# Retention and a gated FFN: another order for the first loads and the first items

## The chip, the cores and the metric

The kernel runs on one core of a Trainium2 chip. The metric is the device time of one execution in microseconds (us), the median of several runs.

## The reference

Causal retention (attention without softmax, with a decay per head), then two matrix products with `h - tanh(h)` between them:

```python
scores = scale * np.matmul(q, k.transpose(0, 1, 3, 2))        # batch 8, heads 8, seq 576, head_dim 64
Dmat = np.where(rel >= 0, gamma[:, None, None] ** rel[None, :, :], 0.0)   # rel = row - column
attn = np.matmul(scores * Dmat[None], v)
x = attn.transpose(0, 2, 1, 3).reshape(4608, 512)
h = x @ w_in                                                  # 512 x 2048
out = (h - np.tanh(h)) @ w_out                                # 2048 x 512
```

All inputs and outputs are float32.

## The kernel before, in words

The sequence is cut into nine chunks of 64 positions. One batch entry of one chunk is an *item*; eight items (a *chunk*) give a block of 512 tokens for the FFN. The chunks are linked by a state for each batch entry. The FFN works on one block and one tile of 128 hidden units (f, 16 of them) at a time: `mm1` makes a tile h_f by 12 matmuls of 512 columns, `mm2` adds a tile's part to the output.

Every float32 operand of the FFN is split into two words, a high word (`xh`, `gh`) cast on ScalarE and a low word (`xl`, `gl`) that VectorE makes by subtraction; a product is three matmuls. A weight tile is split with more care: it is loaded (`load_w`, 512 KB, tile name rwi), *guarded* (two activations on ScalarE, L106 and L111, into a mask), put together in three VectorE operations (L137, L145, L147; for weight tile 1, in `second`, L124, L126, L127), cast to its high word on ScalarE (L153, L129) and subtracted for the low word (L166). In the text w0, w1, w2 are the weight tiles 0, 1, 2. `unit` is this work for one tile, cut by `yield` into steps that `step()` runs one at a time; `finish` issues the low word that is left over.

The start handles the items of chunk 0 (0 to 7). Each is one load of 384 KB (`load_first`, tile name a). TensorE makes its scores (s_first), VectorE multiplies them by the decay (pm, L308), TensorE makes the output (own_first), ScalarE casts it to xh (L326), VectorE subtracts for xl (L329). Scores of item j+2 are interleaved with the output of item j by `run`. All eight items are needed before h_0, the first FFN tile. Ahead of them TensorE runs *fillers*: matmuls on a zero tile (`busy`, L553).

From chunk 3 on, chunks go in pairs through `stage_a`, which makes an FFN block's products from seven combined weight and input variants (`product`), for pairs j of hidden tiles. Its sums go through `u2` and `u4` on VectorE to c22, c12 and c21, with one piece of the first pair (`rest`) left for the second pair in a list, `pending`.

The order is written by hand: `in_order` ties each engine's instructions to the order in which the code issues them. All loads but two go out on SP's queue, strictly in order, over eight completion semaphores (DMAHW0 to 7). Some loads are *paced*: `paced` notes the instruction issued last, and `behind` makes a load wait until that instruction is done.

Of the kernel before, what the change touches and what calls it, by code (L numbers as in the profile page):

```python
# [13 lines left out]
AF = mybir.ActivationFunctionType  # L14
ALU = mybir.AluOpType
PSUM = bass.MemoryType.PSUM

B, H, S, D = 8, 8, 576, 64
# [11 lines left out]


STEP = float(np.arctanh(0.5) / (1.06 * 2.0**-15))
WARM = 24

NI = NC * B
NV = 7
# [38 lines left out]
def retention_ffn(ctx: ExitStack, tc: tile.TileContext, ins, out, spill, wvar):  # L75
# [36 lines left out]

    halves = (slice(0, DM // 2), slice(DM // 2, DM))

    def second(low):

        t, f = stream[1]
        hw, lw, z = wraw[t, f][:, :, 1], wraw[t, f][:, :, 0], masks.pop((t, f))
        del wraw[t, f]

        w = const.tile([P, 2, 2, DM // 2], F32R, tag="wi14", name="wi1")
        win[f] = w
        upto("guard", 3)
        nc.vector.scalar_tensor_tensor(z, hw, 3, z, op0=ALU.logical_shift_left, op1=ALU.bitwise_and)  # L124
        low()
        nc.vector.scalar_tensor_tensor(z, lw, 29, z, op0=ALU.logical_shift_right, op1=ALU.bitwise_or)  # L126
        nc.vector.scalar_tensor_tensor(z, hw, -0x40000000, z, op0=ALU.bitwise_and, op1=ALU.bitwise_or)  # L127
        for n, at in enumerate(halves):
            nc.scalar.copy(w[:, n, 0], z[:, at].bitcast(F32))  # L129
        last.append(("i", w, z))  # L130
# [32 lines left out]
    def finish():  # L163
        while last:
            hi, lo, full = words_of(*last.pop())
            nc.vector.tensor_tensor(lo, full, hi.bitcast(F32), op=ALU.subtract)  # L166
# [7 lines left out]
    def upto(what, n):  # L174
        while at_[what] < min(n, 2 * NF):
            {"load": load_w, "guard": guard}[what](*stream[at_[what]])
            at_[what] += 1
# [106 lines left out]
    def m_out(j, o, state_last=False):  # L284
        c0, b = divmod(j, B)
        a, pm = loaded[j], scored[j]
        ms = []
        for i in range(4):
            two = [[(o[half(1 - c), i], a[half(c), 2, i, :], pm[half(c), i, :]) for c in range(2)]]
            if c0 > 0:  # L290
                two.insert(state_last, [(o[half(1 - c), i], state[half(c), b, i, :], a[half(c), 0, i, :]) for c in range(2)])
            ms += [(*m, k == 0, k == len(two) - 1) for k, terms in enumerate(two) for m in terms]
        return ms

    def run(same, other):

        while same or other:
            for ms in (same, other):
                for out_, w, x, start, stop in ms[:2]:
                    nc.tensor.matmul(out_, w, x, start=start, stop=stop)  # L300
                del ms[:2]

    def after_score(j, sc, n):

        if j < B:

            pm = pool.tile([P, 2, 4, C], F32, tag="gh", name=f"pm{j}")
            nc.vector.tensor_tensor(pm[:, 0], sc[:, 0], decay, op=ALU.mult)  # L308
        else:

            pm = parts[j, 0][:, :, 1]
            nc.vector.tensor_tensor(
                pm, sc, mask.unsqueeze(1).unsqueeze(1).broadcast_to([P, n, 4, C]), op=ALU.mult,
            )
        for u in range(n):
            scored[j + u] = pm[:, u]
# [234 lines left out]
    def busy(n, cols):  # L551
        for _ in range(n):
            nc.tensor.matmul(wps[:, :cols], warm[:, :P], warm[:, :cols], start=True, stop=True)  # L553

    busy(WARM, 140)
    busy(8, BLK // 2)
    decay = const.tile([P, 4, C], F32, tag="wo7", name="decay")
    krows = [const.tile([P, 4, 4, D], F32, tag=f"wo{4 + t}", name=f"krows{t}") for t in range(2)]

    def load_first(j, queue=nc.sync):  # L560
        loaded[j] = const.tile([P, 3, 4, C], F32, tag=f"wo{NF - 1 - j}", name=f"a{j}")
        queue.dma_start(loaded[j], first_d[j])

    load_first(0)
    nc.scalar.dma_start(decay, decay_d)
    load_first(1, nc.scalar)
    load_first(2)
    upto("load", 1)
    load_first(3)
    load_first(4)  # L570
    load_first(5)
    nc.scalar.activation(warm[:, :1], warm[:, :1], AF.Tanh)

    firsts, lows = {}, []

    def score_first(j):
        firsts[j] = psp.tile([P, 8, C], F32, tag=("o0", "o1", "h")[j % 3], bufs=(1, 1, 2)[j % 3], name=f"s_first{j}")
        firsts[j] = firsts[j][:, :4]  # L580
        return m_score(j, firsts[j])

    def paced(load):

        pace.append(tc.nc.cur_bb.bb.instructions[-1].name)
        load()

    def load_paced(j):
        load_first(j)
        behind(tc, pace[-1])  # L590

    run(score_first(0), [])
    after_score(0, firsts[0].unsqueeze(1), 1)
    run(score_first(1), [])
    after_score(1, firsts[1].unsqueeze(1), 1)
    for j in range(B):
        o = psp.tile([P, 8, C], F32, tag=("o2", "o3", "own")[j % 3], bufs=1, name=f"own_first{j}")[:, :4]
        run(score_first(j + 2) if j < B - 2 else [], m_out(j, o))
        if j == 0:
            paced(lambda: load_paced(6))  # L600
        if j == 1:
            paced(lambda: load_paced(7))
        if j < B - 2:
            after_score(j + 2, firsts[j + 2].unsqueeze(1), 1)
            if 0 < j < 5:
                paced(lambda: upto("load", j + 1))
        if j == 4:
            nc.sync.dma_start(vtab, vtab_d)
            nc.sync.dma_start(krows[0], krows_d[0])
            load_pair(B)  # L610
            nc.sync.dma_start(mask, mask_d)
            upto("load", 7)
            load_pair(B + 2)
        if j == 3:
            busy(6, BLK)
        if 0 < j < 4:
            step()
        low = after_out(j, o.unsqueeze(1), 1, False)
        if j == 0:
            upto("guard", 1)  # L620
        if j == 3:
            step()
        if j == 5:
            finish()
            guard(*stream[1], both=False)
        if j < 7:
            low()
        else:
            guard_end(masks[stream[1]])
            at_["guard"] = 2  # L630
    units(1)
    second(low)
    at_["convert"] = 2

    def scale_k(t):
# [319 lines left out]
    def stage_a(na):  # L955

        nb, pending = na + 1, []
        u2, u4 = work[:, 0], work[:, 1]
        for j in range(NPAIR):
            x, y = [psp.tile([P, BLK], F32, tag=t, bufs=1, name=f"p{t}{na}_{j}") for t in ("new" if j else "o0", "own")]  # L960
            z, v = [psp.tile([P, BLK], F32, tag="h", bufs=2, name=f"p{t}{na}_{j}") for t in "zv"]
            f1, f2 = 2 * j, 2 * j + 1
            c22, c12, c21 = [pool.tile([P, BLK], F32, tag="g", bufs=3, name=f"c{t}_{na}_{j}") for t in (22, 12, 21)]

            def tanh(c):
                th = pool.tile([P, BLK], F32, tag="cv", bufs=4, name=f"th{na}_{j}")
                nc.scalar.activation(th, c, AF.Tanh)  # L967
                return th

            def away(c, f):  # L970
                nc.gpsimd.tensor_tensor(c, c, tanh(c), op=ALU.subtract)  # L971
                nc.sync.dma_start(spill[nb, f], c)

            product(0, x)
            product(1, y)
            nc.scalar.copy(u2, x)
            nc.vector.tensor_tensor(u2, y, u2, op=ALU.add)  # L977
            product(2, z)
            nc.vector.tensor_tensor(u4, z, u2, op=ALU.add)
            while pending:  # L980
                pending.pop()()
            product(3, v)
            nc.vector.tensor_tensor(c22, v, u4, op=ALU.add)  # L983
            y = psp.tile([P, BLK], F32, tag="own", bufs=1, name=f"py{na}_{j}")
            product(4, y)
            away(c22, f2)
            nc.vector.tensor_tensor(c12, y, u4, op=ALU.add)
            product(5, x, False)
            away(c12, f1)
            g11 = tanh(x)  # L990
            nc.vector.tensor_tensor(g11, x, g11, op=ALU.subtract)
            product(6, v, False)
            split(na, f1, g11, False)
            nc.vector.tensor_tensor(c21, v, u2, op=ALU.add)

            def rest(f=f2, c=c21, tanh=tanh):
                nc.vector.tensor_tensor(c, c, tanh(c), op=ALU.subtract)
                split(na, f, c, True)

            if j == 0:  # L1000
                pending.append(rest)
            else:
                mm2_pair(na, j - 1)
                rest()
        for f in range(3):
            fetch(nb, f)
        mm2_pair(na, NPAIR - 1)
        for f in range(2):
            split(nb, f, fetched.pop((nb, f)), False)
# [123 lines left out]
```

## Time and profile before

| | us |
|---|---|
| median of 3 runs (lowest to highest) | 854.9 (854.4 to 855.17) |
| profiled execution | 856.53 |
| its span, first to last instruction | 854.8 |
| TensorE busy in the span | 843.2 |
| VectorE busy | 484.6 |
| ScalarE busy | 364.4 |

In the profile's rows PE is TensorE's matmuls, PEld its weight loads, DVE VectorE, ACT ScalarE, SPq the queue that issues loads. A row of the timeline has the start, the time taken, the engine, the line, the operation with output and inputs, and in brackets how long the engine stood idle before it and what ended that. A row of a group has its count and the mean time of one. A row of DMA issues has the size and the time from issue to landing. Line numbers are those of the kernel before; in the changed kernel they lie up to ten lower.

### The profile page before, as it was taken

How to read it: one execution, taken by the hardware profiler on the slowest of the kernel's cores; microseconds unless marked ns; L12 is line 12 of the kernel's file. 1: busy time of each engine (PE TensorE's matmuls, PEld its weight loads, DVE VectorE, ACT ScalarE, POOL GpSimd, SP SyncE). 2: the span in 40 equal slices, each digit the busy share in tenths (PEclk: the TensorE clock that was granted, in tenths of full speed). 3: DMA queues.
4: the chain of work that ended last, by engine and by line, in shares of the span. 5: the costliest groups of instructions: out<-in, count | busy, mean ns of one | idle time of the engine just before them, and what ended most of it. 6: DMA issues, size and time to landing. Idle time of an engine off the chain costs nothing.

```text
span 854.8 us, 18569 instructions
## 1 busy us (share of the span) xinstructions
PE 843.2 (99%) x7701; PEld 695.2 (81%) x7702; DVE 484.6 (57%) x817; ACT 364.4 (43%) x723; POOL 74.3 (9%) x63
## 2 busy tenths in 40 slices
PE   7999999999999999999999999999999999999998
PEld 6888888887888787888888788888888888888886
DVE  5989877868567665434346754434456554343321
ACT  4887774444234553323244443322345433232321
POOL 0001001110000001212110002211100012121100
PEclk9999999999999999999999999999999999999999
DMA  9976968776777579435376665534666255352432
GB/s 340 364 244 205 365 222 277 239 235 202 234 259 289 188 252 326 163 130 190 123 235 213 205 184 199 182 132 173 208 207 215 90 184 185 128 192 74 138 109 74
DMA packets 62404, 174.67 MB, mean 204 GB/s; under 512 B 7536, under 2 KB 8944, under 8 KB 57072
## 3 DMA queue, kind: packets, MB, share of 16 engines
q1 hardware_dynamic: 61792, 172.57, 59.5%
q8 instruction: 60, 0.98, 0.5%
q10 hardware_dynamic: 528, 0.92, 0.3%
q14 instruction: 24, 0.20, 0.1%
HBM read 124.70 MB, written 48.76 MB: 203 GB/s over the span
## 4 chain that ended last, share of the span: by engine, by line
PE 87%; issue 4%; DMA 4%; DVE 2%; ACT 1%; SPq 0%; POOL 0%; DVEq 0%; POOLq 0%; ACTq 0%
PE o L503 25%; PE o L948 15%; PE h L447 15%; PE pv L917 7%; PE pnew L917 6%; PE py L917 4%; PE pz L917 4%; PE pown L917 4%; PE s L300 3%; DMA s<-spill_dram 2%; PE new L300 2%; PE own L300 2%; DMA a<-in_first_dram 1%; PE po L917 1%; DMA rwi<-in_w_in_dram 1%
## 5 line engine op out<-in xcount | busy, mean ns | idle before, releaser
L503 PE MATMUL o<-wo,gh 128*128 128x512 f32 x608 | 156.8, 395 | 0.3 <-ACT gh L484 0.3
L503 PEld LDWEIGHTS o<-wo,gh 128*128 128x128 f32 x608 | 111.8, 188 | 26.8 <-ACT gh L484 2.2
L971 POOL TENSOR_TENSOR c<-c,th 128x512 f32<-128x512 f32 x48 | 62.0, 1297 | 516.6 <-ACT th L967 515.5
L967 ACT ACTIVATE th<-c 128x512 f32<-128x512 f32 x72 | 45.5, 632 | 140.9 <-DVE c L983 89.7
L447 PE MATMUL h<-xh,wi 128*128 128x512 f32 x384 | 97.7, 392 | 0.8 <-ACT xh L326 0.5
L447 PEld LDWEIGHTS h<-xh,wi 128*128 128x128 f32 x384 | 71.3, 188 | 16.9 <-ACT wi L129 0.8
L503 PE MATMUL o<-wo,gl 128*128 128x512 f32 x304 | 84.2, 389 | 0.0
L948 PE MATMUL o<-wo,gs 128*128 128x512 f32 x288 | 70.7, 389 | 0.0
L503 PEld LDWEIGHTS o<-wo,gl 128*128 128x128 f32 x304 | 57.1, 188 | 11.9
L948 PEld LDWEIGHTS o<-wo,gs 128*128 128x128 f32 x288 | 54.1, 188 | 11.2
L917 PE MATMUL pv<-xhv,ws 128*128 128x512 f32 x192 | 59.2, 390 | 0.6 <-DVE c L983 0.6
L503 PE MATMUL o<-wo,gs 128*128 128x512 f32 x240 | 59.2, 394 | 0.0
L300 PE MATMUL own<-qk,state 64*64 64x64 f32 x928 | 57.1, 221 | 0.0
L300 PE MATMUL own<-qk,vr 64*64 64x64 f32 x928 | 56.1, 218 | 0.7 <-issue 0.7
L977 DVE TENSOR_TENSOR work<-pown,work 128x512 f32<-128x512 f32 x24 | 16.6, 692 | 67.8 <-PE pown L917 67.1
L503 PEld LDWEIGHTS o<-wo,gs 128*128 128x128 f32 x240 | 44.4, 188 | 9.5
L917 PE MATMUL pnew<-xhv,ws 128*128 128x512 f32 x168 | 51.7, 389 | 0.0
L447 PE MATMUL h<-xl,wi 128*128 128x512 f32 x192 | 51.6, 389 | 0.0
L948 PE MATMUL o<-wo,gh 128*128 128x512 f32 x192 | 48.9, 389 | 0.0
L300 PEld LDWEIGHTS own<-qk,vr 64*64 64x64 f32 x928 | 46.6, 135 | 0.1
L300 PEld LDWEIGHTS own<-qk,state 64*64 64x64 f32 x928 | 46.2, 134 | 0.4 <-issue 0.4
L933 DVE TENSOR_TENSOR gl<-s,gh 128x512 fp32r<-128x512 f32 x44 | 30.0, 688 | 23.9 <-ACT gh L932 12.1
(152 smaller groups left out, 1516.4 us busy)
## 6 DMA issues: line engine op xcount, KB each, us to landing
ws<-wvar_dram SPq DMA_DIRECT2D x41, 1024.0 KB, 4.7
s<-spill_dram SPq DMA_DIRECT2D x94, 256.0 KB, 3.8
qk<-in_qkv_dram SPq DMA_DIRECT2D x29, 512.0 KB, 4.2
vr<-in_qkv_dram SPq DMA_DIRECT2D x29, 512.0 KB, 3.9
spill_dram<-c SPq DMA_DIRECT2D x48, 256.0 KB, 2.3
spill_dram<-g SPq DMA_DIRECT2D x36, 256.0 KB, 3.5
rwi<-in_w_in_dram SPq DMA_DIRECT2D x16, 512.0 KB, 5.6
rwo<-in_w_out_dram SPq DMA_DIRECT2D x16, 512.0 KB, 5.5
```

The source lines that it names most:

```text
L300: nc.tensor.matmul(out_, w, x, start=start, stop=stop)
L447: nc.tensor.matmul(hp, win[f][:, cc // 2, a, cc % 2 * P : (cc % 2 + 1) * P], x[:, cc, :], start=(k == 0), stop=(k == 3 * NCC - 1))
L503: nc.tensor.matmul(ops[n][t], g[:, t * P : (t + 1) * P], wout[f_][:, a, :], start=(f_ == first and k == 0), stop=(f_ == final and k == 2),)
L917: nc.tensor.matmul(into, w[:, a, k], x[:, k], start=start and i == 0, stop=i == len(terms) - 1, skip_group_check=not start,)
L933: nc.vector.tensor_tensor(gl, g, gh.bitcast(F32), op=ALU.subtract)
L948: nc.tensor.matmul(ops[n][t], g[:, t * P : (t + 1) * P], wout[f][:, a, :], start=(j == 0 and f == fs[0] and k == 0), stop=last_,)
L967: nc.scalar.activation(th, c, AF.Tanh)
L971: nc.gpsimd.tensor_tensor(c, c, tanh(c), op=ALU.subtract)
L977: nc.vector.tensor_tensor(u2, y, u2, op=ALU.add)
```

## The change

Six edits. At the start, weight tile 0 is loaded first of all on SP and items 0 to 5 behind it, all on SP's queue (item 1 was on ScalarE's); the order was item 0, item 2, weight tile 0, items 3 to 5. The fillers ahead of the items become 11 of 512 columns instead of 24 of 140 and 8 of 256, and the 6 fillers after item 3's output go. Weight tile 0's guard and conversion steps move ahead of and between items 0 to 2. Item 7's scores are issued whole, ahead of item 5's output, instead of interleaved with it. The pacing marks move: they are taken before `after_score` instead of behind it. A tanh on one column that loaded ScalarE's table early goes, and the low word of each item is issued at once. In `stage_a`, c22 is computed ahead of what is pending, and `u2` alternates between two places.

```diff
-WARM = 24
+WARM = 11
...
-    busy(WARM, 140)
-    busy(8, BLK // 2)
+    busy(WARM, BLK)
...
-    load_first(0)
+    upto("load", 1)
     nc.scalar.dma_start(decay, decay_d)
-    load_first(1, nc.scalar)
-    load_first(2)
-    upto("load", 1)
-    load_first(3)
-    load_first(4)
-    load_first(5)
-    nc.scalar.activation(warm[:, :1], warm[:, :1], AF.Tanh)
...
+    for j in range(6):
+        load_first(j)
+    upto("guard", 1)
...
     run(score_first(0), [])
+    step()
     after_score(0, firsts[0].unsqueeze(1), 1)
     run(score_first(1), [])
+    step()
     after_score(1, firsts[1].unsqueeze(1), 1)
     for j in range(B):
         o = psp.tile([P, 8, C], F32, tag=("o2", "o3", "own")[j % 3], bufs=1, name=f"own_first{j}")[:, :4]
-        run(score_first(j + 2) if j < B - 2 else [], m_out(j, o))
-        if j == 0:
-            paced(lambda: load_paced(6))
-        if j == 1:
-            paced(lambda: load_paced(7))
-        if j < B - 2:
-            after_score(j + 2, firsts[j + 2].unsqueeze(1), 1)
-            if 0 < j < 5:
-                paced(lambda: upto("load", j + 1))
+        if j == 5:
+            run(score_first(7), [])
+            run([], m_out(j, o))
+        else:
+            run(score_first(j + 2) if j < B - 2 else [], m_out(j, o))
+        if j < 2:
+            paced(lambda: load_paced(6 + j))
+        if 0 < j < 5:
+            paced(lambda: upto("load", j + 1))
...
-        if j == 3:
-            busy(6, BLK)
-        if 0 < j < 4:
+        if j == 0:
             step()
-        low = after_out(j, o.unsqueeze(1), 1, False)
+        if j < B - 2:
+            after_score(j + 2, firsts[j + 2].unsqueeze(1), 1)
+        after_out(j, o.unsqueeze(1), 1)
         if j == 0:
-            upto("guard", 1)
-        if j == 3:
             step()
+        if j == 1:
+            finish()
...
-        u2, u4 = work[:, 0], work[:, 1]
+        u4 = work[:, 1]
         for j in range(NPAIR):
+            u2 = work[:, 3 * (j % 2)]
...
+            product(3, v)
+            nc.vector.tensor_tensor(c22, v, u4, op=ALU.add)
             while pending:
                 pending.pop()()
-            product(3, v)
-            nc.vector.tensor_tensor(c22, v, u4, op=ALU.add)
```

Three places in the engines' order. First SP's queue, which issues the loads, from item 6 on, before (a_161 and a_190 are items 6 and 7, rwi_194 to rwi_244 the weight tiles 1 to 3; what a load waits for stands in brackets):

```order
L562 DMA a_161<-in_first_dram 128x768 [waits DMAHW0_49,PE_49]
L562 DMA a_190<-in_first_dram 128x768 [waits DMAHW1_49,PE_49]
L96 DMA rwi_194<-in_w_in_dram 128x1024 [waits DMAHW2_49,DVE_49]
L96 DMA rwi_219<-in_w_in_dram 128x1024 [waits DMAHW3_49,DVE_49]
L96 DMA rwi_244<-in_w_in_dram 128x1024 [waits DMAHW4_49,DVE_49]
```

The same place of the change (a_144 and a_173 are items 6 and 7, rwi_175 to rwi_224 the weight tiles 1 to 3):

```order
L560 DMA a_144<-in_first_dram 128x768 [waits DMAHW0_49,PE_49]
L560 DMA a_173<-in_first_dram 128x768 [waits DMAHW1_49,PE_49]
L96 DMA rwi_175<-in_w_in_dram 128x1024 [waits DMAHW2_49,DMAHW1_49]
L96 DMA rwi_200<-in_w_in_dram 128x1024 [waits DMAHW3_49,PE_49]
L96 DMA rwi_224<-in_w_in_dram 128x1024 [waits DMAHW4_49,PE_49]
```

The loads stand in the same order; weight tile 1 waited for a VectorE instruction and now waits for DMAHW1, on which the load of item 7 reports (weight tile 0's was the one before it there), and tiles 2 and 3 wait for TensorE instead of VectorE.

Second, ScalarE behind item 5's output, before (xh_165 is the block's high word, mi_320 the mask of weight tile 1) and then of the change (xh_149, mi_293):

```order
L326 CAST xh_165<-own_first_298 128x4x64 [waits PE_49]
L106 ACTIVATE mi_320<-rwi_194 128x512 [waits DMAHW2_49]
L326 CAST xh_165<-own_first_323 128x4x64 [waits PE_49]
L326 CAST xh_165<-own_first_334 128x4x64 [waits PE_49]
L111 ACTIVATE mi_320<-mi_320 128x512 [waits Activation_49]
```

```order
L325 CAST xh_149<-own_first_271 128x4x64 [waits PE_49]
L106 ACTIVATE mi_293<-rwi_175 128x512 [waits DMAHW2_49]
L325 CAST xh_149<-own_first_295 128x4x64 [waits PE_49]
L325 CAST xh_149<-own_first_306 128x4x64 [waits PE_49]
L111 ACTIVATE mi_293<-mi_293 128x512 [waits Activation_49]
```

Nothing moved here: in both, the guard of weight tile 1 stands ahead of the casts of items 6 and 7.

Third, VectorE in the second pair (1) of the first `stage_a`, before and of the change (c_3_0_4089 and c_3_0_4061 are the first pair's c21, c_3_1_4160 and c_3_1_4132 the second pair's c22):

```order
L977 TENSOR_TENSOR work<-pown_1_4157,work 128x512 [waits PE_49,Activation_49]
L979 TENSOR_TENSOR work<-pz_1_4158,work 128x512 [waits DVE_49,PE_49]
L997 TENSOR_TENSOR c_3_0_4089<-c_3_0_4089,th_1_4186 128x512 [waits Activation_49]
L933 TENSOR_TENSOR gs<-c_3_0_4089,gs 128x512 [waits Activation_49]
L983 TENSOR_TENSOR c_3_1_4160<-pv_1_4159,work 128x512 [waits DVE_49,PE_49]
```

```order
L968 TENSOR_TENSOR work<-pown_1_4129,work 128x512 [waits PE_49,Activation_49]
L970 TENSOR_TENSOR work<-pz_1_4130,work 128x512 [waits DVE_49,PE_49]
L972 TENSOR_TENSOR c_3_1_4132<-pv_1_4131,work 128x512 [waits DVE_49,DMAHW5_49,PE_49,Pool_49]
L988 TENSOR_TENSOR c_3_0_4061<-c_3_0_4061,th_1_4165 128x512 [waits Activation_49]
L923 TENSOR_TENSOR gs<-c_3_0_4061,gs 128x512 [waits Activation_49]
```

c22 moved ahead of the two pending instructions, and now also waits for the store of the first pair's c22 out of its buffer.

More of the change, by code (lines that the diff above doesn't have):

```diff
@@ L113, in retention_ffn, with second @@
     halves = (slice(0, DM // 2), slice(DM // 2, DM))
-    def second(low):
+    def second():
         t, f = stream[1]
@@ L124, in second @@
         nc.vector.scalar_tensor_tensor(z, hw, 3, z, op0=ALU.logical_shift_left, op1=ALU.bitwise_and)
-        low()
         nc.vector.scalar_tensor_tensor(z, lw, 29, z, op0=ALU.logical_shift_right, op1=ALU.bitwise_or)
@@ L562, in load_first @@
         queue.dma_start(loaded[j], first_d[j])
-    load_first(0)
+    upto("load", 1)
     nc.scalar.dma_start(decay, decay_d)
-    load_first(1, nc.scalar)
-    load_first(2)
-    upto("load", 1)
-    load_first(3)
-    load_first(4)
-    load_first(5)
-    nc.scalar.activation(warm[:, :1], warm[:, :1], AF.Tanh)
-    firsts, lows = {}, []
+    for j in range(6):
+        load_first(j)
+    upto("guard", 1)
+    firsts = {}
     def score_first(j):
@@ L613, in retention_ffn @@
             load_pair(B + 2)
-        if j == 3:
-            busy(6, BLK)
-        if 0 < j < 4:
+        if j == 0:
             step()
-        low = after_out(j, o.unsqueeze(1), 1, False)
+        if j < B - 2:
+            after_score(j + 2, firsts[j + 2].unsqueeze(1), 1)
+        after_out(j, o.unsqueeze(1), 1)
         if j == 0:
-            upto("guard", 1)
-        if j == 3:
             step()
+        if j == 1:
+            finish()
         if j == 5:
-            finish()
             guard(*stream[1], both=False)
[L626 to L632, printed above, removed]
+    guard_end(masks[stream[1]])
+    at_["guard"] = 2
+    assert not going and not last
+    second()
     at_["convert"] = 2
```

## The prediction

> **What bounds the kernel now.** I read the page first, then who TensorE waits for, then the chain of waits through the start, then single stretches of the engines.
>
> ```profile
> PE 843.2 (99%) x7701; PEld 695.2 (81%) x7702; DVE 484.6 (57%) x817; ACT 364.4 (43%) x723; POOL 74.3 (9%) x63
> q8 instruction: 60, 0.98, 0.5%
> qk<-in_qkv_dram SPq DMA_DIRECT2D x29, 512.0 KB, 4.2
> spill_dram<-c SPq DMA_DIRECT2D x48, 256.0 KB, 2.3
> ```
>
> TensorE is busy for 99% of the span, so an edit pays only where TensorE stands still. The waits of TensorE over the whole span (us in total, times, longest) say where that is:
>
> ```profile
> PE s_first L300 <- DMA a<-in_first_dram: 2.9, 5, 1.3
> ...
> PE pv L917 <- DVE c L983: 0.6, 1, 0.6
> PE h L447 <- ACT xh L326: 0.5, 1, 0.5
> PE h L447 <- ACT wi L129: 0.3, 1, 0.3
> ```
>
> All but one lie in the first 20 us; the other, for c22, is the one that the last hunk of the diff touches. What sets the end of the start? The chain of waits (start, us, what):
>
> ```profile
> 2.13 6.55 DMA a<-in_first_dram
> ...
> 9.59 0.44 DVE pm L308
> 10.04 5.13 DMA rwi<-in_w_in_dram
> 15.20 0.68 ACT mi L106
> 15.88 0.54 ACT xh L326 x2
> 16.41 0.54 ACT mi L111
> 16.98 0.69 DVE mi L124
> 17.67 0.33 DVE xl L329
> 18.00 0.61 DVE mi L126
> 18.64 0.70 DVE mi L127
> 19.36 0.41 ACT wi L129
> 19.82 3.01 PE h L447 x12
> 22.84 5.79 PE h L447 x24
> ```
>
> This is not the chain of weight tile 0. It is that of weight tile 1 (w1): loaded from 10.04, landed at 15.17, guarded on ScalarE, put together by three operations of VectorE, cast, and used by h_1 at 19.82. From there TensorE runs on without a gap, so the start of h_1 is what has to come earlier. TensorE's own timeline before it:
>
> ```profile
> 14.05 0.27 PE L300 MATMUL s_first<-a 64*64 64x64 f32 x2 [0.41 <-DMA a<-in_first_dram]
> ...
> 14.52 1.44 PE L300 MATMUL own_first<-pm,a 64*64 64x64 f32 x34
> 16.47 2.11 PE L447 MATMUL h<-xh,wi 128*128 128x512 f32 x8 [0.51 <-ACT xh L326]
> 18.42 1.07 PE L447 MATMUL h<-xl,wi 128*128 128x512 f32 x4
> ```
>
> h_0 starts at 16.47, 1.30 after w1 landed, and that is no accident: on ScalarE the first guard of w1 (15.20) stands ahead of the casts xh of items 6 and 7, so h_0 cannot start before w1 has landed either.
>
> **The change part by part.** *Tile 0 first, items behind it.* Only the order of the first 3.8 MB changes. Ahead of item 3 there were decay, items 0 to 2 and w0, and there still are, so item 3 lands at 8.68 as in the chain's first row. Item 0 lands later by w0's 512 KB, and w0 earlier; its guard and its three VectorE operations move into the waits for items 0 to 2, where VectorE has room. What w0 was late for was nothing: h_0 waited for xh. Worth 0, and hidden by the loads of the items.
>
> *The load of w1.* Here is the price. Before, its issue waited for VectorE's third pm (9.59 plus 0.44, hence 10.04). Now the pacing mark is taken right behind the load of item 7, so the mark is that load, and w1 may not be issued before item 7 has landed. The loads of w2, w3, w4 and all that SP issues later are queued behind it on SP, ScalarE's casts of items 6 and 7 behind w1's guard, and h_0 and h_1 behind those. When does item 7 land, and how long does w1 then take? SP's issues of items 6 and 7, the landing time of item 6, and all transfers up to 12.0 us:
>
> ```profile
> 8.16 0.33 SPq L562 DMA_DIRECT2D a<-in_first_dram  x1
> ...
> 9.58 0.33 SPq L562 DMA_DIRECT2D a<-in_first_dram  x1
> ...
> a<-in_first_dram SPq DMA_DIRECT2D x1, 384.0 KB, 3.5
> ...
> DMA packets 1431, 3.82 MB, mean 318 GB/s; under 512 B 153, under 2 KB 281, under 8 KB 1430
> q8 instruction: 1, 0.02, 0.6%
> ```
>
> Item 7 is issued when item 1's output is computed, behind item 3's landing: 9.6 in both. Late bound of its landing: 14.05, where TensorE got it before. Early bound: by 12.0 us 3.82 MB had moved, and decay, w0 and eight items are 3.80 MB, so its bytes were nearly all across; item 6 landed at 8.16 + 3.5 = 11.66, and 384 KB at 318 GB/s take 1.2, which gives 12.9. That it took 1.1 longer I put down to the one instruction packet in the window: the page has 60 of them, 0.98 MB, for 15,403 instructions of TensorE, so 16 KB, some 257 instructions, and a packet occupies one of 16 engines. It comes by count. Now 54 TensorE instructions fewer stand ahead (21 fillers of two fewer at the start, 6 in the middle), which puts it into item 4's run, behind most of item 7's bytes. So I take 13.1, nearer the early bound.
>
> w1 then meets an idle queue. The nearest rows are the loads of 512 KB later in the program, median 4.2 for qk on the page, and for vr:
>
> ```profile
> DMA to landing us min/median/max: 3.3/3.9/8.1
> ```
>
> Bounds 3.3 and 4.2; I take 3.6, since nothing else is in flight. w1 lands at 13.1 + 3.6 = 16.7 (early 12.9 + 3.3 = 16.2, late 14.05 + 4.2 = 18.25), against 15.17.
>
> The Trainium skill, "DMA: Bandwidth & Descriptors", section "Anatomy of one DMA", gives a fixed 2.0 us plus the bytes over 436 GB/s, of which most is the receipt after the last byte. By it w1 would take an estimated 3.2, and the sum below would come out 0.4 lower; the shortest row here, 3.3, agrees with it nearly.
>
> From w1's landing to h_1 it was 19.82 - 15.17 = 4.65. The xl at 17.67 now stands ahead of the chain; two spacings of 0.70 (18.64 to 19.34) take the place of 1.02 and 0.64 behind L124, so about 0.2 goes: 4.45. h_1 starts at 16.7 + 4.45 = 21.15, later by **1.3** (early 20.65, +0.8; late 22.7, +2.9). h_0 starts at 16.7 + 1.3 = 18.0 and ends 2.85 later, just ahead of h_1, so it is not the bound. Since TensorE has no gap behind h_1 that could take this in, it stays to the end. w2 to w4 now go out in a row behind w1, and VectorE needs four operations of 0.69 for a tile against TensorE's 5.79 for two, so the tiles stay ahead.
>
> *Item 7's scores ahead of item 5's output, six fillers gone.* TensorE waits for w1 in both; scores earlier make pm 7 earlier, 0 on the path. The same for the warm-up: 24 of 140 and 8 of 256 columns are 5,408, 11 of 512 are 5,632, and item 0 now lands after the fillers' end.
>
> *c22 sooner.* The second pair of the first variant stage, VectorE and then TensorE:
>
> ```profile
> 337.78 0.68 DVE L997 TENSOR_TENSOR c<-c,th 128x512 f32<-128x512 f32 x1
> 339.15 0.69 DVE L933 TENSOR_TENSOR gs<-c,gs 128x512 fp32r<-128x512 f32 x1 [0.69 <-ACT gs L932]
> 339.95 0.69 DVE L983 TENSOR_TENSOR c<-pv,work 128x512 f32<-128x512 f32 x1
> ...
> 339.08 0.62 PE L917 MATMUL pnew<-xlv,ws 128*128 128x512 f32 x2
> 339.53 0.61 PE L917 MATMUL pnew<-xhv,ws 128*128 128x512 f32 x2
> 340.69 0.73 PE L917 MATMUL pv<-xhv,ws 128*128 128x512 f32 x2 [0.55 <-DVE c L983]
> 341.26 0.63 PE L917 MATMUL pv<-xlv,ws 128*128 128x512 f32 x2
> ```
>
> Pairs of matmuls follow each other by 0.45 (339.08, 339.53); the pair at 341.26 was due at 340.44, so the wait costs 0.8. With c22 first it takes L997's place at 337.8 and is done at 338.5, 1.5 us before it is needed. It now also waits for the first pair's c22 to leave its buffer: that was made seven products of 1.36 earlier, and the store takes 2.3 (the page), which leaves 7 us for the tanh and the subtraction between: 0. The gs behind it moves to about 340.4, and mm2 needs it at 342.2 less 0.7: covered by 1.1. The second home for u2 takes a wait of ScalarE's copy away that TensorE does not see: 0. **-0.8**, in this stage alone; the waits list has no second one.
>
> **Sum.** +1.3 - 0.8 = +0.5. The profiled execution took 856.53 us, 854.8 of it the span; its time becomes 857.0. It lies 1.6 above the median of the three runs, 854.9, so the median becomes **855.4**.
>
> **The rivals.** *TensorE goes cold before h_0 (slower).* The place is the wait between item 7's output and h_0. Item 7's scores to the last output took 14.05 to 15.96, so the new idle time reaches from about 15.0 to 18.0, 3 us, with no filler left in it; before it was 0.5. What a slow clock costs is in the fillers:
>
> ```profile
> 1.19 3.86 PE L553 MATMUL wps<-warm 128*128 128x140 bf16 x32 [1.19 <-DVE warm L547]
> ...
> 11.53 1.24 PE L553 MATMUL wps<-warm 128*128 128x512 bf16 x5 [0.16 <-issue]
> ```
>
> The later ones stream 2,560 columns in 1.24, 2.1 per ns; the first 5,408 took 3.86, 1.4 per ns, which half speed for some 2.8 us and full speed for the rest would make (an estimate). For h_0's matmuls of 0.23 half speed adds 0.2 each, over 2.8 us up to all 12: 1.3 to 2.4, less the 0.3 by which h_0 ends ahead of h_1. With 1.5 the sum is +2.0: 856.9. It decides once an idle time is long enough for the drop; the longest here, 1.3 us in the waits for items, did no harm, and no row shows a longer one: chance 0.12. The Trainium skill, "TensorE: Matmul & The Clock Gate", section "Part 1: The HAM clock gate", speaks against the change here: a free-running window of about 3.4 us that is idle halves the clock. By it 3 us would still pass, narrowly, and 855.4 would stand.
>
> *Item 7 lands as late as before, and w1 takes the median (slower).* The instruction packet hits the same transfer: +2.9 - 0.8 = +2.1, 857.0. For it: 14.05 is the only landing that was seen. Chance 0.10.
>
> *All is early (same).* +0.8 - 0.8 = 0.0: 854.9, and 854.5 with the spread of the runs. Part of the forecast's side, 0.2.
>
> *c22 sooner does nothing*, since something else than the order on VectorE held it: +1.3, 856.2. The spacing of VectorE's rows speaks against it: 0.06.
>
> *Faster.* 1.7 us would need w1 in place before 14.5, which the wait for item 7 excludes, or a gain in a stage where TensorE does not wait. I see none: 0.08.
>
> **How the numbers follow.** Forecast 0.44, with all-early and c22-without-effect 0.70; these lie within 0.2% (1.7 us), about what a measurement can tell. Slower by more: 0.12 + 0.10 = 0.22. Faster: 0.08. The range goes from 854.0, below the early case by the runs' spread, to 857.6, which takes in the late case and most of the cold one.
>
> **What would show it.** Right: w1's issue directly behind item 7's landing, near 13; DMA engines idle between 13 and 14; h_0 at about 18 and h_1 at about 21; the wait for c22 gone. Wrong: w1's issue near 10, or h_1 before 20.5; a lower spacing than 0.23 in h_0 would be no cold clock, 0.43 would be one; a wait of pv in the second pair that is still there.

## The result and the profile after

The changed kernel takes 859.3 us (median of six runs, 858.3 to 863.6), the kernel before 854.4 us on the same chip (854.0 to 855.2). The ratio is 1.0056, with a 95% interval of 1.0038 to 1.0074: **slower by about half a percent**. The prediction, 855.4 with a range of 854.0 to 857.6, was wrong. The profiled execution of the change took 858.73 us, 856.9 of it the span, against 856.53 and 854.8 before.

TensorE's row on the first part of the page of the change shows that no work was added; the waits of TensorE (us in total, times, longest) show what was:

```profile
PE 842.8 (98%) x7675; PEld 695.2 (81%) x7675; DVE 484.4 (57%) x817; ACT 365.6 (43%) x722; POOL 75.4 (9%) x63
```

```profile
PE s_first L299 <- DMA a<-in_first_dram: 3.4, 7, 1.5
PE h L446 <- ACT xh L325: 2.6, 1, 2.6
PE new_first L299 <- issue: 1.5, 1, 1.5
...
PE new L299 <- issue: 0.9, 2, 0.6
```

Two rows stand out. The wait of h for the cast xh was 0.5 and is 2.6. The wait at new_first, 1.5 us with no releaser that the profile shows ("issue"), did not exist. The row of pv behind c22 (0.6 before) is gone. The waits for items grew from 2.9 to 3.4.

The chain of waits through the start of the change (start, us, what):

```profile
9.95 4.27 DMA a<-in_first_dram
...
14.24 3.61 DMA rwi<-in_w_in_dram
...
17.87 0.66 ACT mi L106
18.53 0.54 ACT xh L325 x2
19.07 0.04 issue
19.11 12.80 PE h L446 x48
```

Item 7 lands at 14.22, and w1 is issued in the same moment, at 14.24; before it was issued at 10.04. Its load takes 3.61 and lands at 17.85. Then comes the guard, the casts, and h_0 at 19.11. But the chain does not go on as before. There it went through the VectorE work on w1 to h_1. Here it enters TensorE at h_0 and stays: 12.80 us for 48 matmuls, so TensorE itself is late. The one-microsecond windows say why (core; from:to; busy time and instructions of PE, PEld, DVE, ACT, POOL; then granted clock, DMA share, GB/s):

```profile
13.00:14.00 1.00, 0.00 (x0) 0.00 (x0) 0.76 (x2) 0.30 (x1) 0.00 (x0) 1.00 0.06 22
14.00:15.00 1.00, 0.64 (x28) 0.67 (x29) 0.00 (x0) 0.00 (x0) 0.00 (x0) 1.00 0.00 0
...
17.00:18.00 1.00, 0.00 (x0) 0.00 (x0) 0.00 (x0) 0.13 (x1) 0.00 (x0) 1.00 0.98 393
...
19.00:20.00 1.00, 0.89 (x3) 0.76 (x4) 0.95 (x3) 0.59 (x2) 0.00 (x0) 0.81 1.03 410
20.00:21.00 1.00, 1.00 (x3) 0.72 (x3) 0.97 (x2) 0.75 (x2) 0.00 (x0) 0.50 0.98 393
...
22.00:23.00 1.00, 1.00 (x4) 0.81 (x3) 0.82 (x2) 1.00 (x3) 0.00 (x0) 0.50 1.03 394
23.00:24.00 1.00, 1.00 (x5) 0.80 (x5) 0.96 (x3) 0.97 (x3) 0.00 (x0) 0.98 1.02 397
```

Three things stand in these rows. From 13 to 15 the DMA engines do nearly nothing, which is the hole ahead of w1. In the 17:18 window TensorE does nothing. And half a microsecond after h_0 begins, at 19.63, the granted clock falls to 0.50 and stays there until 23.04. TensorE's timeline shows what that does to h_0, and when h_1 begins (at 23.57):

```profile
19.11 3.37 PE L446 MATMUL h<-xh,wi 128*128 128x512 f32 x8 [2.57 <-ACT xh L325]
22.28 1.44 PE L446 MATMUL h<-xl,wi 128*128 128x512 f32 x4
23.57 0.62 PE L446 MATMUL h<-xh,wi 128*128 128x512 f32 x2
```

Eight matmuls take 3.37 where they took 2.11. From the start of h_0 to that of h_1 it is 4.46, against 3.35 before.

Following the same matmul through both traces, the change is later by 2.65 us at h_0, by 3.75 at h_1, by about 5 behind the stall at new_first, by 2.65 at 339 us, since pauses of 0.2 to 0.7 at other places fall differently in the two executions, by 1.78 behind c22, and by 2.2 at the end of the span. The medians lie 4.9 apart. The profiled execution of before was itself 2.1 slower than the median of the six runs, and that of the change 0.6 faster than its own, so the two traces show less than half of the loss.

### The profile page after: what moved, and what is told of

Same layout as the page of the kernel before. It is cut to its first block, busy times and chain, and to the rows that moved or that the text cites. A ratio compares the mean times of both kernels' runs of the same rounds, so it can differ in the third digit from the quotient of the medians.

```text
span 856.9 us, 18511 instructions
## 1 busy us (share of the span) xinstructions
PE 842.8 (98%) x7675; PEld 695.2 (81%) x7675; DVE 484.4 (57%) x817; ACT 365.6 (43%) x722; POOL 75.4 (9%) x63
## 4 chain that ended last, share of the span: by engine, by line
PE 97%; DMA 2%; issue 0%; ACT 0%; SPq 0%
PE o L502 31%; PE h L446 16%; PE o L938 15%; PE pv L907 8%; PE pnew L907 7%; PE py L907 4%; PE pz L907 4%; PE pown L907 4%; PE s L299 3%; PE new L299 2%; PE own L299 2%; DMA a<-in_first_dram 1%; PE po L907 1%; PE new_first L299 0%; DMA rwi<-in_w_in_dram 0%
```

## The experiments

The two theories were these. **A**: the time went where the prediction put it, into the load of w1 that now waits for item 7, only more of it. **B**: the clock fell, because TensorE had too little to do before h_0, through that wait or through the six fillers that are gone. A third cause joined them after the first profiles: **C**, the new stall at new_first, from instructions that arrive late. All ratios are against the kernel before on the same chip, with 95% intervals. Each run lists the mean granted clock of every execution, and that counts the drops roughly: 3.4 us at half speed take 0.002 off it, and a drop in the last 2 us of the kernel up to 0.001 more. The profiles with one stretch at half speed ahead of that have 0.997 or 0.998, those with two 0.996, those with three 0.994 or 0.993.

### e1_mark: the change, with w1 issued as early as before

```diff
-        if 0 < j < 5:
+        if j == 1:
+            upto("load", 2)
+        if 1 < j < 5:
             paced(lambda: upto("load", j + 1))
```

> The change, but the load of weight tile 1 (w1) is marked by item 1's output on TensorE, not by item 7's load. Theory A (w1's wait for item 7's landing is the cause, the cold clock follows from it): w1 issued near 10.4, landed near 15.4, h_0 at 16.7, h_1 at 19.9, clock 1.00 throughout, and with c22 sooner 0.9 below before: 853.5 us, ratio 0.999. Theory B (the fillers that were taken out let the clock drop, whatever w1 does): the granted clock still drops to 0.5 around h_0, some 856 to 858 us, ratio 1.002 to 1.004.

Measured: 1.0045 (1.0029 to 1.0061), no better than the change. The edit did what it says: w1 was issued at 10.52. But item 7 now landed at 15.66, and w1 at 16.92. The waits of TensorE and two-microsecond windows of e1_mark:

```profile
PE s_first L299 <- DMA a<-in_first_dram: 5.8, 8, 2.8
...
PE new_first L299 <- issue: 1.9, 1, 1.9
```

```profile
12.00:14.00 2.00, 0.69 (x32) 0.59 (x32) 1.73 (x5) 0.73 (x2) 0.00 (x0) 1.00 0.87 237
14.00:16.00 2.00, 0.21 (x4) 0.24 (x6) 0.00 (x0) 0.00 (x0) 0.00 (x0) 0.56 0.85 284
16.00:18.00 2.00, 2.00 (x48) 2.00 (x48) 0.55 (x2) 0.55 (x2) 0.00 (x0) 0.50 0.95 371
...
20.00:22.00 2.00, 2.00 (x8) 1.53 (x8) 1.84 (x3) 1.26 (x3) 0.00 (x0) 0.73 1.06 396
```

TensorE waits up to 2.8 for an item, has 0.69 and 0.21 us of work in four, and the clock falls ahead of item 7's scores. It stays low from 14.25 to 21.07. Behind the stall at new_first it fell a second time, from 55.21 to 58.62. So A alone is not it: with w1 out of its wait the loss is the same, and the profile has the clock and the stall in its place. Every one of its ten executions had a mean clock of 0.998 or less, and here the times go with it: the five at 0.997 or 0.998 took 857.0 to 859.9, the five at 0.996 or less 859.9 to 862.6. In e9_late and e10_change, below, no such order shows.

### e2_fill: the change, with twelve fillers ahead of h_0

```diff
     second()
+    busy(12, BLK)
```

> The change, with 12 fillers of 512 columns (2.6 us) between item 7's output and h_0; w1 still waits for item 7's landing. Theory A: h_0 stays at 19.1, warm; h_1 goes from 23.6 to 22.3 (w1's landing 17.9 plus 4.45); 2.5 late less 0.9: some 856.0, ratio 1.002. Theory B: the whole loss goes, 853.5 to 854.4, ratio 0.999 to 1.000.

Measured: 1.0048 (1.0032 to 1.0064). h_0 ran warm here (its eight matmuls took 2.19), yet nothing was won, and the trace says why: the clock had already fallen at 15.24, in the wait for item 7, where no filler stood; item 7's outputs ran at half speed, and the twelve fillers behind them ended at 20.5 us, where w1's landing at 18.30 plus the 1.26 that h_0 takes from it in the change would have made 19.56. The fillers held h_0 back themselves by a microsecond. Two of the four executions had a mean clock of 0.999 and 1.000, and they took 860.4 and 859.5, no less than the others. The run does not tell A from B; its twelve fillers are used again in e8_warm, where the clock is held from the beginning.

### e3_wait: the kernel before, with w1 behind item 7

```diff
             paced(lambda: load_paced(7))
+            paced(lambda: upto("load", 2))
...
-            if 0 < j < 5:
+            if 1 < j < 5:
                 paced(lambda: upto("load", j + 1))
```

> The kernel before with one edit: w1's load waits for item 7's landing. All fillers stay, the six after item 3 too. Theory A: w1 lands near 17.8, the idle time before h_0 is some 2 to 3 us and the clock drops in part of the runs: h_1 at 22.3 to 23.6, 856.9 to 858.2, ratio 1.003 to 1.0045. Theory B: the six fillers hold the clock, and what is left is the late tile alone: at most 856.9, no row of the clock below 1.00.

Measured: 1.0053 (1.0033 to 1.0074), the whole loss of the change from this one edit, in four executions. All fillers of before are there. The waits of TensorE in e3_wait:

```profile
PE h L447 <- ACT xh L326: 4.6, 1, 4.6
```

w1 was issued at 14.90 and landed at 20.22, h_0 began at 21.49 after 4.6 us without work, the clock was 0.5 from 18.77 to 25.60, and h_1 began at 26.25.

### e4_c22: the kernel before, with the second pair's c22 sooner

```diff
-        u2, u4 = work[:, 0], work[:, 1]
+        u4 = work[:, 1]
...
+            u2 = work[:, 3 * (j % 2)]
...
+            product(3, v)
+            nc.vector.tensor_tensor(c22, v, u4, op=ALU.add)
             while pending:
                 pending.pop()()
-            product(3, v)
-            nc.vector.tensor_tensor(c22, v, u4, op=ALU.add)
```

> The kernel before with the last hunk alone (c22 ahead of what is pending, u2 in two places). If the order on VectorE held c22: the wait of pv for c22 in the second pair is gone, 0.8 to 0.9 less: 853.5, ratio 0.999. If something else held it: the wait stays, ratio 1.000.

Measured: 1.0002 (0.9992 to 1.0013). The wait of pv for c22 is gone from its list, and the same matmul's distance from the kernel before shrinks by 0.86 us at 339 us. In the change it shrinks by 0.87; VectorE's row there, and TensorE's (start, length):

```profile
340.19 0.69 DVE L972 TENSOR_TENSOR c<-pv,work 128x512 f32<-128x512 f32 x1 [0.74 <-PE pv L907]
```

```profile
342.18 0.61 PE L907 MATMUL pnew<-xhv,ws 128*128 128x512 f32 x2
342.63 0.62 PE L907 MATMUL pv<-xhv,ws 128*128 128x512 f32 x2
```

c22 is done at 340.88, and the pairs of matmuls follow each other by 0.45 without a hole. 0.86 us is 0.1%, and the interval is as wide as that, so the time can't show it. The gain is not always there to be had, either: in e3_wait, where c22 stands in its old place, the wait is not in the list at all, since TensorE came to that place later against VectorE. VectorE's row of e3_wait, and TensorE's:

```profile
343.63 0.69 DVE L984 TENSOR_TENSOR c<-pv,work 128x512 f32<-128x512 f32 x1
```

```profile
343.74 0.61 PE L918 MATMUL pnew<-xhv,ws 128*128 128x512 f32 x2
344.38 0.73 PE L918 MATMUL pv<-xhv,ws 128*128 128x512 f32 x2
```

There c22 and the last pair before it end within 0.03 us of each other, where before the pair ended 0.5 sooner.

### e5_count: the change, its warm-up columns cut into as many fillers as before

The change issues 54 TensorE instructions fewer. Here the 5,632 columns of warm-up are 38 fillers of 148, so the count of instructions is that of before.

```diff
-    busy(WARM, BLK)
+    busy(38, 148)
```

> The change with 38 fillers of 148 columns at the start instead of 11 of 512: as many columns, and as many TensorE instructions as the kernel before. Theory C (part of the loss is a stall of TensorE's instruction stream: with 54 instructions fewer a border of 16 KB falls into the short matmuls near 53 us): the idle time of 1.5 us before new_first is gone, 1.5 less than the change; w1 still waits and the clock still drops. If the count does not matter: the idle time stays near 53 us.

The stall is gone. The chain of waits by line, from 50 to 60 us, in the change and then in e5_count:

```profile
by line: PE h L446 54.4%; issue 15.5%; PE new_first L299 11.8%; PE s L299 8.8%; PE new L299 7.2%; PE own L299 4.3%
```

```profile
by line: PE h L446 72.8%; PE new_first L299 9.2%; PE s L299 8.8%; PE new L299 7.2%; PE own L299 4.3%
```

1.55 us of "issue" have become matmuls. The time did not follow: 1.0048 (1.0029 to 1.0067). Its profile had two stretches at half speed in the start (13.94 to 17.35 and 20.76 to 24.18), a w1 that took 5.3 us, and h_1 only at 25.35. So C exists, but 1.5 us are 0.18%, and the intervals are that wide. A clock that falls behind the stall, as in e1_mark, would add to its price; in the two profiles of the change it did not.

### e6_all: the change, with w1 early, the six fillers back and the count of before

```diff
-    busy(WARM, BLK)
+    busy(32, 176)
...
-        if 0 < j < 5:
+        if j == 1:
+            upto("load", 2)
+        if 1 < j < 5:
             paced(lambda: upto("load", j + 1))
+        if j == 3:
+            busy(6, BLK)
```

> The change with three things mended: w1 marked by item 1's output, the six fillers of 512 columns back after item 3, and 32 fillers of 176 columns at the start (TensorE's count as before). What is left of the change is the order of the first loads, w0's conversion ahead, item 7's scores whole, c22 sooner. Theory A+B+C (late w1, cold clock and instruction border are the whole loss): clock 1.00, h_1 near 19.8 or somewhat earlier, and 0 to 0.9 below before, ratio 0.999 to 1.000. If the order of loads and of w0's conversion costs something itself: above 1.002 with a clock of 1.00.

Measured: 1.0001 (0.9988 to 1.0014). The loss is gone. What is left of the change in it is the order of the loads, w0's conversion ahead, item 7's scores before item 5's output, wider warm-up fillers and c22: together no gain and no loss that the interval of 0.13% to either side would show. The waits of TensorE in e6_all:

```profile
PE s_first L299 <- DMA a<-in_first_dram: 2.7, 7, 0.9
...
PE h L446 <- ACT xh L325: 0.5, 1, 0.5
```

No clock below 1.00 in the start of its profile, and a mean clock of 0.999 or more in 11 of 12 executions. h_1 began at 20.75, later than before by 0.9, since item 7 landed at 14.81 and w1 at 16.12; that is as much as c22 gives back.

### e7_nosix: the kernel before, without the six fillers

```diff
     busy(WARM, 140)
     busy(8, BLK // 2)
+    busy(6, 16)
...
-        if j == 3:
-            busy(6, BLK)
```

The six narrow fillers keep the count of instructions.

> The kernel before without the six fillers after item 3; six of 16 columns at the start keep TensorE's count. w1 is not late. Theory B (the six fillers hold the clock through the items): the granted clock drops to 0.5 for one or two stretches of 3.4 us between 13 and 22 in most executions, +1 to +4 us, ratio 1.001 to 1.005. If they only fill a wait: clock 1.00, ratio 1.000.

Measured: 1.0006 (0.9991 to 1.0021). The clock does fall without them. Windows of e7_nosix:

```profile
12.00:14.00 2.00, 0.81 (x32) 0.75 (x32) 1.60 (x5) 0.62 (x1) 0.00 (x0) 0.88 0.83 248
14.00:16.00 2.00, 1.92 (x54) 1.85 (x52) 1.46 (x4) 0.83 (x3) 0.00 (x0) 0.50 0.94 322
16.00:18.00 2.00, 1.53 (x22) 1.29 (x19) 1.15 (x4) 1.78 (x5) 0.00 (x0) 0.77 0.94 320
```

It was 0.5 from 13.51 to 16.92, and 7 of 10 executions had a mean clock of 0.998 or less, against 4 of 25 of the kernel before beside them. But the slow stretch fell on the items' 64-wide matmuls and ended before h_0, at 17.49, which ran at full speed, 2.11 for its eight matmuls; h_0 and h_1 both began a microsecond later than before, as in e6_all, where the clock held. This drop cost little. The one of e1_mark lasted into h_0 and beyond it.

### e8_warm and e9_late: w1 late, with the clock held and without

Both have the six fillers and the count of before, and both let w1 wait for item 7, as the change does. e9_late is e6_all with the wait put back, and nothing else; the two ran on different chips, so they are compared by their ratios. e8_warm, on the chip of e9_late, has twelve fillers more ahead of h_0, and as many fewer but longer ones at the start.

e8_warm, against the change:

```diff
-    busy(WARM, BLK)
+    busy(20, 282)
...
+        if j == 3:
+            busy(6, BLK)
...
     second()
+    busy(12, BLK)
```

> The change with w1 still waiting for item 7's landing, but TensorE kept busy: 20 fillers of 282 columns at the start, the six of 512 back after item 3, and 12 of 512 ahead of h_0; TensorE's count of instructions as before. Theory A (w1's lateness costs by itself, without the clock): clock 1.00, w1 lands near 18, h_1 at 22.3 to 22.9, 2.5 to 3 later than in the kernel before, less 0.85 for c22: ratio 1.002 to 1.0025. If the clock and the instruction border are the whole loss: ratio 0.999 to 1.000.

e9_late, against the change:

```diff
-    busy(WARM, BLK)
+    busy(32, 176)
...
+        if j == 3:
+            busy(6, BLK)
```

> As the kernel with all three things mended (e6_all), but w1 waits for item 7's landing again: the one edit between the two is the wait. Theory A: h_0 near 20 behind some 2.5 us of idle time, the clock drops in part of the executions, h_1 at 22.5 to 25: 2 to 4 above e6_all, ratio 1.002 to 1.005. Rival (the fillers after item 3 hold the clock through this wait too): clock 1.00 and ratio 1.002 to 1.0025, as e8_warm.

Measured: e8_warm 1.0021 (1.0006 to 1.0035), e9_late 1.0048 (1.0031 to 1.0065). The waits of TensorE and the windows, e8_warm first:

```profile
PE h L446 <- ACT xh L325: 1.6, 1, 1.6
```

```profile
18.00:20.00 2.00, 1.60 (x8) 0.52 (x6) 0.00 (x0) 0.06 (x1) 0.00 (x0) 1.00 0.92 340
20.00:22.00 2.00, 0.82 (x4) 0.68 (x5) 1.06 (x3) 2.00 (x5) 0.00 (x0) 1.00 1.03 397
```

and e9_late:

```profile
PE h L446 <- ACT xh L325: 3.5, 1, 3.5
```

```profile
18.00:20.00 2.00, 0.00 (x0) 0.00 (x0) 0.00 (x0) 0.87 (x3) 0.00 (x0) 0.93 0.92 356
20.00:22.00 2.00, 1.62 (x4) 1.34 (x5) 1.83 (x4) 1.97 (x5) 0.00 (x0) 0.50 1.03 401
...
24.00:26.00 2.00, 2.00 (x6) 1.61 (x5) 1.97 (x4) 1.08 (x3) 0.00 (x0) 0.50 1.04 401
```

In e8_warm the fillers end at 19.6, h_0 begins at 21.18, 1.27 after w1 landed (19.91), at clock 1.00, and h_1 at 24.34. In e9_late w1 landed sooner, at 19.11, and h_0 began sooner, at 20.38, but h_1 came at 25.66. From w1's landing to h_1 that is 4.43 warm and 6.55 cold, 2.1 us for the clock. Over the executions: in e8_warm 8 of 10 had a mean clock of 0.999 or more, in e9_late none of 7. The ratios split the loss: 0.2% (1.7 us) for the late w1, with c22's gain in it, and 0.27% (2.3 us) for the clock. The two intervals overlap a little, so the split is good to a microsecond or two. In its profile e8_warm has h_1 4.5 later than before, 3.7 with c22's gain, which is more than that 1.7; that execution was 1.3 slower than the median of its run.

### e10_change: the change again, beside e8_warm and e9_late

> The change itself once more, beside the two others on one chip: ratio 1.004 to 1.007, clock 0.994 to 0.998. All theories alike; e9_late lies below it by the instruction border (1.5 us, 0.0018) and by the clock's drop within the items.

Measured: 1.0046 (1.0029 to 1.0062), which e9_late equals. Its profile shows the same things, in other sizes. The waits of TensorE and the windows:

```profile
PE s_first L299 <- DMA a<-in_first_dram: 5.7, 8, 2.9
PE new_first L299 <- issue: 2.0, 1, 2.0
PE h L446 <- ACT xh L325: 1.9, 1, 1.9
```

```profile
14.00:16.00 2.00, 0.15 (x3) 0.18 (x5) 0.00 (x0) 0.00 (x0) 0.00 (x0) 0.66 0.04 11
16.00:18.00 2.00, 2.00 (x46) 2.00 (x48) 0.49 (x2) 0.37 (x1) 0.00 (x0) 0.50 0.63 170
```

Item 7 landed at 15.72 this time, the clock was 0.5 from 14.64 to 24.88, and h_1 began at 25.67. In 15 executions of the change, in both runs together, the mean clock was 0.998 or less each time; of the 21 of before beside e10_change 18 had 0.999 or more.

The profiles of the runs together, us from the span's start (the last column begins with the clock's first rise, at 4 to 7, and leaves out the last 2 us):

```
             item 7   w1 issued -> landed    h_0     h_1    w1 landed to h_1   clock 0.5
before        13.91    10.04 -> 15.18       16.47   19.82        4.64          never
e4_c22        14.28     9.95 -> 15.56       16.84   20.19        4.63          never
e6_all        14.81    10.21 -> 16.12       17.61   20.75        4.63          never
e7_nosix      14.04    10.17 -> 15.89       17.49   20.84        4.95          13.5-16.9
e1_mark       15.66    10.52 -> 16.92       19.58   23.13        6.21          14.3-21.1, 55.2-58.6
change        14.22    14.24 -> 17.85       19.11   23.57        5.72          19.6-23.0
e10_change    15.72    15.74 -> 19.77       21.04   25.67        5.90          14.6-24.9
e2_fill       14.60    14.62 -> 18.30       20.54   23.47        5.17          15.2-18.7
e3_wait       14.88    14.90 -> 20.22       21.49   26.25        6.03          18.8-25.6
e5_count      14.46    14.48 -> 19.79       21.06   25.35        5.56          13.9-17.4, 20.8-24.2
e9_late       14.52    14.53 -> 19.11       20.38   25.66        6.55          19.7-26.6
e8_warm       14.59    14.61 -> 19.91       21.18   24.34        4.43          never
```

No version beats the kernel before; e6_all equals it.

## Why the prediction was wrong

**The order of the loads, worth 0: right.** e6_all keeps it and comes out at 1.0001.

**The load of w1: right in mechanism, too small in size.** That w1 would wait for item 7, with an idle DMA in between, and that w2 to w4, the casts, h_0 and h_1 would stand behind it, is what the trace shows. The +1.3 was wrong in two terms. Item 7 was taken to land at 13.1, and landed at 14.22, outside the bounds of 12.9 to 14.05; in the other runs with this wait it came at 14.46 to 15.72. And the load of w1 was put at 3.6 (3.3 to 4.2): the profile of the change has 3.61, but the six other runs took 3.68 to 5.32. The rows from which it was taken were of loads later in the program; the row of w1 itself, 5.13 before, was set aside because other loads ran beside it. No run came down to the 3.2 that the prediction worked out from the Trainium skill, "DMA: Bandwidth & Descriptors", section "Anatomy of one DMA", which gives its formula for loads that GpSimd issues; these go out on SP. The term behind w1's landing, 4.45 to h_1, was right for a warm TensorE: 4.43 in e8_warm.

The step behind the 13.1 was that the instruction packet "comes by count", so that 54 instructions fewer would put it behind item 7's bytes. That failed. From 13 to 14 us in the change the DMA view by queue has this, with 5.6% of 16 engines, which is 0.9 us of one:

```profile
q1 hardware_dynamic: 10, 0.02, 5.6%
```

In the single records the first engine reports item 7 done at 12.62, the fifteenth at 13.68 and the last at 14.22. The 16 KB packet of instructions runs from 11.22 to 12.24, and pieces of item 7 follow it end to end up to 13.73, where the last of them is through. Nine of the twelve profiles show such a row of pieces from the packet to item 7's last one, the kernel before among them. In every run the last engine is 1.5 to 2.9 us behind the first. The packet was fetched between 10.1 and 12.9 us: at 11.22 in the change, at 12.04 in e10_change, which is the same kernel, and at 12.94 in e1_mark, which issues just the same TensorE instructions. What sets its moment was not found. The loads of w1 may have the same reason for their spread: in e3_wait, e5_count and e8_warm, where they took 5.3, the next packet was fetched at 17.6 to 18.0, and the last engine was 1.7 to 1.8 us behind the fifteenth; in the change and e2_fill, with 3.6 and 3.7, it was fetched at 17.0 and 17.1. That is not shown.

**Six fillers gone, "0 on the path": wrong, and put at 0 without a reason.** They stood in a wait and cost nothing, but they kept the clock. Without them it fell in 7 of 10 executions (e7_nosix) and cost little there; e1_mark differs from e6_all by them and by the count of instructions alone, and the two stand at 1.0045 and 1.0001. How much of that is the fillers and how much the stall that comes with the count, with the second drop of the clock behind it, was not told apart.

**TensorE goes cold before h_0: the rival that came true, and the step that failed.** The prediction gave its place, its sign (0.43 as the spacing in h_0; in the change 3.37 us for eight is 0.42) and its price, 1.5 on h_1. Measured, from w1's landing to h_1: 5.72 in the change and up to 6.55, against 4.43 held warm, so 1.3 to 2.1. What failed was its chance, 0.12, and that the sum put the clock at nothing. The chance rested on an idle time of 1.3 that did no harm, and 3 us were taken to pass. The idle time in the change was 2.57, shorter than the 3 us of that rival, and the clock fell. The Trainium skill, "TensorE: Matmul & The Clock Gate", section "Part 1: The HAM clock gate", was read as a rule that needs some 3.4 us with nothing in them. The stretches at half speed agree with its window: 3.41 us, or two or three times that (6.8 in e9_late, 10.2 in e10_change). The reading of "idle" does not agree: TensorE had 0.85 us of matmuls in the 3.41 us before the drop in the change, and 1.59 in e1_mark, short 64-wide ones. Windows of the change (two) and of e1_mark:

```profile
12.80:16.21 3.41, 1.86 (x66) 1.69 (x61) 1.66 (x4) 0.74 (x2) 0.00 (x0) 1.00 0.30 79
16.21:19.63 3.42, 0.85 (x14) 0.67 (x11) 0.76 (x4) 1.72 (x4) 0.00 (x0) 1.00 0.96 365
```

```profile
10.83:14.25 3.42, 1.59 (x79) 1.21 (x69) 2.90 (x8) 1.12 (x3) 0.00 (x0) 1.00 0.90 276
```

What the prediction should have counted is TensorE's work in 3.41 us, not the longest gap; the last section has the figures.

The two bad terms were also not independent. The prediction summed the late w1 and held the cold clock apart as another case, though the same wait makes both: each microsecond by which w1 is late is a microsecond without work ahead of h_0. A term that adds idle time should have carried the clock's price with it.

**c22, -0.8: right.** It was 0.87 in the trace of the change. It is too small to be told from nothing in the times. The sentence that all waits but this one lie in the first 20 us holds for the rows shown there; the full list of the kernel before also has 1.2 us of "issue" at own and new, and smaller waits at o and two.

**The sum.** Predicted +0.5; the medians differ by 4.9, the ratio of the second run is 0.46%, 3.9 us. For the profiled execution the forecast was 857.0, and it took 858.73. The last step of the sum, 1.6 off from the profiled execution to the median, did not carry over: the change's profiled execution lies below its median. Of the 3.9 e8_warm leaves 1.7 (0.5 to 3.0) without the clock, in which +0.5 stands at the lower end; the clock's 2.3 is the part that was not in the forecast. The stall at new_first, 1.5 to 2.0 in three profiles, was not foreseen either; e5_count and e9_late took it away and were no faster, so what it costs in the times stays open.

## What to carry to other kernels

An edit that makes TensorE wait is not paid for by the wait alone: ask how much work is left in each 3.4 us around it, and whether the matmuls behind it set the end of the stage, for then both bills come. A filler in a wait looks free to remove, and is, only as long as the rest of the waits around it leaves the clock up. And a load put behind another load's completion gives up its overlap with it: here an issue 4.2 us later became a landing 2.7 us later in the change, and one 4.4 to 5.7 us later a landing 3.1 to 5.0 us later in the six other runs with the wait.

## What the runs showed of the hardware

The clock falls for 3.41 us or a multiple, on a grid of that step that begins where the clock first rose (at 5.97 in the change, at 4.05 to 7.11 in the others). What decides is how much of a step of this grid TensorE is busy. In the twelve profiles half speed followed sixteen steps at full speed, and in all of them TensorE was busy for 47% of the step or less (ten in the first 56 us, with 11 to 47%; six at the very end of the kernel, where its work runs out). In the other 2,955 steps it was busy for 53% or more, and the clock stayed. So the place of a wait on the grid counts as much as its length: in the change the step from 12.80 to 16.21 had 55% and passed, the next had 25%. At half speed, steps with 21 to 81% were followed by another, those with 86% or more by full speed (fifteen steps in all), so an h_0 that begins well into a cold step brings a second. Twelve fillers of 512 columns held the clock through 4.3 us between item 7's outputs and h_0 in e8_warm, of which 1.6 stayed idle, but narrowly, with 54% (the window's PE column has 1.84):

```profile
18.82:22.24 3.42, 1.84 (x9) 1.05 (x8) 1.30 (x3) 2.29 (x5) 0.00 (x0) 1.00 0.99 381
```

One 16 KB packet of instructions, 0.9 to 1.9 us long in the records of these runs, holds one of the 16 DMA engines, and a load spread over all of them is complete only when that one is: 1.5 to 2.9 us after the first engine was done with item 7.

With 54 TensorE instructions fewer at the start (27 matmuls and their weight loads) a stall of 1.5 to 2.0 us stands in a stretch of short matmuls 40 us later, in the three profiles of the kernels with that count (the change twice and e1_mark). In all three a packet of instructions is fetched there; in the change it runs from 52.44 to 53.36, and TensorE stands still from 53.09. The row behind the stall:

```profile
54.64 1.09 PE L299 MATMUL new_first<-a,krows 64*64 64x64 f32 x30 [1.55 <-issue]
```

The Trainium skill, "Runtime: NRT & Kernel Launch", section "Instruction fetch mechanics", describes fetches in 16 KiB blocks of 256 instructions and calls their cost mostly hidden. The sizes agree (60 packets of 0.98 MB on the page); "hidden" does not hold for this stall, which is in none of the profiles that have the count of before; the longest "issue" wait of the kernel before is 0.7 us.
